# First half's operands made in small pieces between sums, one more sum between two products of each chunk, and two of eight sums on ScalarE in one stage

## The chip, the cores and the metric

The kernel runs on one core of a Trainium2 chip. The engines are named as in the profile: PE is TensorE (PEld its weight loads), DVE VectorE, ACT ScalarE, POOL GpSimd, SP SyncE, whose queue issues most DMAs. The metric is the device time of one execution in microseconds (us), here the median of several runs.

## The reference

Two branches read the same normalized input, and their sum with the input is the output. `q`, `k`, `v` and `x` have 2048 rows of 576 columns.

```python
x  = A_q                              # (1, 2048, 576)
xn = layernorm(x)                     # (x - mean) / sqrt(var + 1e-5), no weights
# branch A: a causal filter of 4 taps on k, times v, a long causal convolution by FFT, gated with xn
kv = sum(k_pad[:, t:t + S] * shift_k[:, ks - 1 - t] for t in range(4)) * v
y  = irfft(rfft(pad(kv)) * rfft(pad(ssm_k)))[:S] + kv * ssm_D
# branch B: an FFN with a hidden width of 4608
h  = maximum(xn @ w1, 0) @ w2
out = x + xn * y + h
```

## The kernel before

**FFN on PE.** The 2048 rows are 16 tiles of 128, in two halves of eight tiles, each half two blocks (`b`) of 512 rows. The hidden width is taken 256 columns at a time. Such a chunk of one half is a *quad*, `g`: 0 to 17 for the first half, 18 to 35 for the second. FP32 operands are split into a high and a low part (ACT copies the high part, DVE or POOL subtracts it), and a product takes three matmuls in place of one. The first two quads are plain (`classical`, four chunks of 14 matmuls each). From quad 2 on (`quad`), the four products of a 2 by 2 block matrix are made by seven (Strassen's scheme, Winograd's form): the x side has the operands `00`, `01`, `11` and the differences `s1` to `s4`, the weight side `wa` to `wd` with `sums`. Each `product` is six matmuls of 512 columns, each `rest` (the last 64 of 576 input columns) two. They are written into two banks, `x` and `y` in `quad`, whose contents ACT and DVE pass on: `u2` and `p5` are copies that the next product is added to, and `hidden` makes the rectified high part (`hh`, ACT) and low part (`ll`, DVE).

Between the products stand the eight *units* of the quad before: `open_unit` takes a PSUM buffer (two in turn), `mm2` multiplies 128 rows of the hidden layer with `w2` in twelve matmuls of 288 columns, and DVE adds the result to `acc`, the 128 by 576 sum of that tile. PE works in program order; where it goes on without a wait, DVE, ACT and POOL have been in time.

**First half's operands.** In the two plain quads the x operands are not yet scaled by `rstd`, which is multiplied in when `acc` is added to. Then `scales` makes a row of the 512 `rstd` values of a block: DVE writes four diagonal matrices, PE multiplies them with ones, ACT copies the row. `scaled` multiplies the operands with it, `combined` makes the differences, `made` and `made_rest` split them. All that is recorded between the plain chunks, in long calls.

**The stream.** `conv` is a generator with branch A and the second half's operands. `tick` is called after each group of matmuls, and gives the stream credit (`rate` times the columns); when it is used up, the next step is recorded. The costs `W_*` say how much credit a step takes, a negative yield is a pause in columns. Its stages: the second half's operands (`later_operands`), the filters' transform (64 `prepare` and `first` steps with `wk`), the taps, gate and first transform of `k` and `v` (`tap`, `gate`, `split`, `first` with `wx`), the middle (`spectrum`, `product_of`, `way_back`, all with `m_sb`), and the way out (`wi`). In the stage of the taps every tile costs DVE seven tap instructions, one gate and two splits. `here()` orders the stream's DVE and ACT work behind the last `acc` and `hh`; a scheduler then sets the order of each engine's instructions.

Of the kernel before, what the change touches and what calls it, by code (L numbers as in the profile page):

```python
# [17 lines left out]
P = 128  # L18
S = 2048
D = 576  # L20
# [44 lines left out]
FFN_TOTAL = (QUADS - PLAIN) * 50 * W_MM + (2 * (QUADS - PLAIN) + 1) * BT * W_UNIT  # L65
# [40 lines left out]
def h3_ffn_kernel(ctx: ExitStack, tc, x, k, v, shift_k, ssm_k, ssm_D, w1, w2, fwd, inv, mid, out):  # L106
# [186 lines left out]
    def scales(pool, b):  # L293

        diag = pool.tile([P, BT, P], F32, tag="diag", name=f"diag{b}")
        for i in range(BT):
            with here():
                nc.vector.tensor_scalar(diag[:, i, :], ident, rstd[:, b * BT + i:b * BT + i + 1],
                                        None, op0=OP.mult)
# [4 lines left out]
        row = pool.tile([P, 512], F32, tag=f"row{b}", name=f"row{b}")  # L304
        with here():
            nc.scalar.activation(row, ps, AF.Copy)
        return row

    def scaled(row, *names):
        for o in names:  # L310
            if isinstance(o, int):
                with here():
                    nc.vector.tensor_tensor(xf[o], xf[o], row[:64], OP.mult)
            else:
                for c in range(2):
                    with here():
                        nc.vector.tensor_tensor(xf[o][:, c, :], xf[o][:, c, :], row, OP.mult)

    def made(o, tag=None):
        dst = operand(o, tag)  # L320
        for c in range(2):
            with here():
                split_chunk(dst, c, xf[o][:, c, :])

    def made_rest(b):
        with here():
            split_rest(rest_operand(b), xf[b])

    def combined(pool, *names):
        for c in range(2):  # L330
            with here():
                combine(pool, xf, names, c)
# [172 lines left out]
    def product(ps, w, off, o, start=False):  # L505

        for c in range(2):
# [5 lines left out]
    def rest(ps, g, b, f):  # L513
        matmuls(ps, [(wr[g][:, n, 0, f * P:(f + 1) * P], hl[b]) for n in range(2)], False)
# [10 lines left out]
    def classical(g, b, f, which, n_low):  # L525
# [19 lines left out]
        hidden(g, b, f, ps)  # L545

    def quad(g, units):
# [16 lines left out]
        product(x, wa[g], 0, "00", start=True)  # L564
# [5 lines left out]
        product(x, wa[g], 2, "01")  # L570
# [7 lines left out]
        product(y, wb[g], 0, "s2")  # L578
# [533 lines left out]
```

## Time and profile before

| | us |
|---|---|
| median of 3 runs | 1096.05 |
| lowest, highest | 1095.46, 1096.5 |
| the profiled execution | 1097.09 |
| its span | 1095.0 |
| PE, PEld busy | 1051.7, 870.8 |
| DVE, ACT, POOL busy | 769.9, 485.5, 457.8 |

The profile is of one execution. Of each engine it tells when an instruction ran, how long the engine sat idle before it, and which instruction on another engine ended that wait. Records of PE overlap, so a PE that is busy need not be at its peak, and the length of a stretch says more than its busy time. Quad 2 starts when PE has done the last plain chunk, at 62.25 us, quad 3 at 99.88. The stage of the filters lies in quads 10 to 15, that of the taps in 16 to 25 (to about 717 us), the middle in 27 to 32.

### The profile page before, as it was taken

To read this page: it belongs to the slowest core of one execution; us is meant where nothing else is said; L and a number is where in the kernel's file an instruction comes from. 1 tells how busy PE (TensorE), PEld (TensorE's weight loads), DVE (VectorE), ACT (ScalarE), POOL (GpSimd) and SP (SyncE) were. 2 spreads that over 40 slices of the span, in tenths; PEclk is the share of its full clock that TensorE was granted. 3 is DMA by queue.
4 is the path that set the end of the run, shared out by engine and by line. 5 is a ranking of instruction groups with operands and counts; after the bars stand their busy time and mean duration, and the time that the engine had idled before them with its cause. 6 is when DMAs were issued, how large, how long until landed. Compare 5 with 4: busy or idle time off the path is not lost. (4 is left out here: it accounts for less than half of the span.)

```text
span 1095.0 us, 17070 instructions
## 1 busy us (share of the span) xinstructions
PE 1051.7 (96%) x6300; PEld 870.8 (80%) x6300; DVE 769.9 (70%) x1149; ACT 485.5 (44%) x929; POOL 457.8 (42%) x496
## 2 busy tenths in 40 slices
PE   8878999999999999798999999999999999999998
PEld 5766899999899998697899899895666665677777
DVE  5787768554887774999999999853444454446765
ACT  7342344333687774344444445434444444432220
POOL 3343454444354444454444445443223223244450
PEclk9989999999999999999999999999999999999999
DMA  6118544992254445589944433237566666457684
GB/s 166 58 38 187 144 150 183 197 154 56 89 160 139 140 140 160 153 259 349 279 134 138 137 114 120 78 138 194 174 197 208 189 209 203 131 179 223 220 248 119
DMA packets 118431, 179.45 MB, mean 164 GB/s; under 512 B 66381, under 2 KB 67551, under 8 KB 116556
## 3 DMA queue, kind: packets, MB, share of 16 engines
q1 hardware_dynamic: 99212, 121.99, 39.3%
q0 software_dynamic: 18816, 55.49, 17.0%
q10 hardware_dynamic: 320, 0.88, 0.3%
q8 instruction: 50, 0.82, 0.3%
q14 instruction: 33, 0.27, 0.1%
HBM read 123.27 MB, written 45.61 MB: 154 GB/s over the span
## 5 line engine op out<-in xcount | busy, mean ns | idle before, releaser
L501 PE MATMUL pso<-w,hh 128*128 128x288 f32 x2304 | 471.4, 297 | 5.4 <-DVE acc L652 3.3
L501 PEld LDWEIGHTS pso<-w,hh 128*128 128x128 f32 x2304 | 381.1, 189 | 36.2 <-issue 8.2
L501 PE MATMUL pso<-w,ll 128*128 128x288 f32 x1152 | 340.4, 295 | 0.0
L656 DVE TENSOR_TENSOR acc<-pso,acc 128x576 f32<-128x576 f32 x272 | 204.6, 753 | 158.0 <-PE pso L501 156.7
L501 PEld LDWEIGHTS pso<-w,ll 128*128 128x128 f32 x1152 | 217.1, 188 | 0.0
L445 POOL TENSOR_TENSOR w<-r,w 128x576 fp32r<-128x576 f32 x72 | 111.5, 1552 | 134.6 <-ACT w L444 134.5
L445 POOL TENSOR_TENSOR wb<-sums,wb 128x512 fp32r<-128x512 f32 x34 | 49.8, 1465 | 203.8 <-ACT wb L444 140.9
L501 PE MATMUL psh<-x,wa 128*128 128x512 f32 x408 | 109.0, 402 | 10.8 <-DVE ll L522 6.5
L501 PE MATMUL psh<-xs,wb 128*128 128x512 f32 x408 | 108.7, 400 | 1.2 <-ACT u L581 1.2
L501 PEld LDWEIGHTS psh<-x,wa 128*128 128x128 f32 x408 | 74.7, 190 | 32.6 <-issue 12.7
L501 PEld LDWEIGHTS psh<-xs,wb 128*128 128x128 f32 x408 | 72.9, 189 | 25.0 <-issue 11.7
L501 PE MATMUL psh<-hl,wr 128*128 128x512 f32 x272 | 88.1, 401 | 1.5 <-ACT psh L604 1.5
L521 ACT ACTIVATE hh<-psh 128x512 fp32r<-128x512 f32 x68 | 40.6, 598 | 91.0 <-PE psh L501 90.7
L604 ACT ACTIVATE psh<-psh 128x512 f32<-128x512 f32 x34 | 19.9, 584 | 132.7 <-DVE u L602 132.7
L445 POOL TENSOR_TENSOR wd<-r,wd 128x256 fp32r<-128x256 f32 x36 | 31.7, 881 | 97.1 <-ACT wd L444 97.1
L522 DVE SCALAR_TENSOR_TENSOR ll<-psh,hh 128x512 fp32r<-128x512 f32 x68 | 46.6, 685 | 34.1 <-ACT hh L521 33.7
L868 DVE TENSOR_TENSOR k<-psf,k 128x512 f32<-128x512 f32 x72 | 44.7, 682 | 36.5 <-PE psf L687 31.6
L676 DVE TENSOR_TENSOR ks<-kt,ks 64x288 fp32r<-64x288 f32 x64 | 54.5, 852 | 18.1 <-ACT ks L675 17.0
L445 POOL TENSOR_TENSOR wa<-r,wa 128x512 fp32r<-128x512 f32 x36 | 51.5, 1430 | 28.8 <-ACT wa L444 28.7
L501 PEld LDWEIGHTS psh<-hl,wr 128*128 128x128 f32 x272 | 46.9, 188 | 19.2 <-issue 12.3
L521 ACT ACTIVATE hh<-p 128x512 fp32r<-128x512 f32 x34 | 21.5, 632 | 90.4 <-DVE p L611 65.4
L501 PE MATMUL psh<-xs,wc 128*128 128x512 f32 x204 | 53.3, 396 | 8.1 <-DVE ll L522 8.1
(146 smaller groups left out, 1642.8 us busy)
## 6 DMA issues: line engine op xcount, KB each, us to landing
r<-in_w POOLq DMA_DIRECT2D x70, 288.0 KB, 3.5
r<-in_w POOLq DMA_DIRECT2D x35, 512.0 KB, 5.2
zk<-zk SPq DMA_DIRECT2D x32, 288.0 KB, 2.6
zx<-zx SPq DMA_DIRECT2D x32, 288.0 KB, 2.7
ztk<-zk SPq DMA_DIRECT2D x18, 512.0 KB, 3.9
ztx<-zx SPq DMA_DIRECT2D x18, 512.0 KB, 3.9
k<-k SPq DMA_DIRECT2D x72, 128.0 KB, 3.2
zy<-vo SPq DMA_DIRECT2D x18, 512.0 KB, 2.6
```

Source lines behind the costliest of these rows:

```text
L445: nc.gpsimd.tensor_tensor(w[:, 1, :n], src, w[:, 0, :n], OP.subtract)
L501: last = nc.tensor.matmul(ps, a, m, start=start and n == 0, stop=n == len(seq) - 1, skip_group_check=True)
L521: done["act"] = nc.scalar.activation(hh, ps, AF.Relu)
L522: nc.vector.scalar_tensor_tensor(ll, ps, 0.0, hh, op0=OP.max, op1=OP.subtract)
L604: nc.scalar.activation(x, y, AF.Copy, scale=-1.0)
L656: done["acc"] = nc.vector.tensor_tensor(two(acc[t]), ps[:, :, :NH], two(acc[t]), OP.add)
L676: nc.vector.tensor_tensor(dst[other], src[own], dst[own], OP.subtract)
L868: nc.vector.tensor_tensor(filt[n][c][:, k, :], banks[k], filt[n][c][:, k, :], OP.mult)
```

## The change

Five things are changed.

1. The eight diagonals are made ahead of the first unit, in buffers of the tag `xn`. The matrix products for the rows stand after two units and after the first chunk of quad 1. The six remaining units of quad 0 stand around the second chunk of quad 1.
2. Scaling, differences and splits of the first half's operands are a generator, `second_half_of_start`, that yields after each piece. `post` records one or two pieces after each unit, four after a plain chunk, until quad 2 is done; `need` records what a product of quad 2 reads ahead of it. Quad 2 is inside the pool `fa` now, so the stream starts after it, one quad later.
3. In every quad unit 3 stands between the products `s2` and `s1`, and unit 4 between `s1` and `s3`.
4. From the stage of the taps up to the middle, units 3 and 4 are *seeded*: ACT copies `acc` into the PSUM buffer, the matmuls add to it, and ACT copies the sum back. DVE has no part in it. There are 26 such units.
5. The stream's costs and pauses have other values.

```diff
-W_FK, W_FX, W_FMK, W_FMX, W_FMB, W_FO = 2.5, 5.8, 2.4, 4.8, 3.4, 6.6
+W_FK, W_FX, W_FMK, W_FMX, W_FMB, W_FO = 2.35, 6.6, 2.4, 4.4, 3.0, 6.0
-KT_GAP = 6000
-N_FB, W_FB = 37, 3.9
+KT_GAP = 4500
+N_FB, W_FB = 37, 4.0
-FFN_TOTAL = (QUADS - PLAIN) * 50 * W_MM + (2 * (QUADS - PLAIN) + 1) * BT * W_UNIT
+FFN_TOTAL = (QUADS - PLAIN - 1) * 50 * W_MM + 2 * (QUADS - PLAIN) * BT * W_UNIT
...
+    def second_half_of_start(pool):
+        for o, b in (("11", 1), ("10", 1), ("00", 0), ("01", 0), (0, 0)):
+            yield from scaled(o, b)
+        yield from combined(pool, "s1")
+        yield from made("s1")
+        yield "00"
+        yield from made("00")
+        yield from combined(pool, "s2")
+        yield from made("s2")
+        yield from made("01")
+        yield from made_rest(0)
+        yield from combined(pool, "s3")
+        yield from made("s3")
+        yield from combined(pool, "s4")
+        yield "10"
+        yield from made("s4")
+        yield from scaled(1, 1)
+        yield from made("11")
+        yield from made_rest(1)
+    def need(g, o):
+        while g == PLAIN and o not in ready:
+            post(1)
...
         def unit(n):
             if n + 1 < len(units):
-                open_unit(*units[n + 1])
+                open_unit(*units[n + 1], n + 1 in stage["seeded"] and more)
             mm2(*units[n])
+            post(2)
...
         nc.scalar.activation(u2, y, AF.Copy)
+        unit(3)
         x = bank(g, 0, "5")
-        product(x, wc[g], 2, "s1", start=True)
+        product(x, wc[g], 2, "s1", start=True, g=g)
...
-        unit(3)
-        product(y, wb[g], 2, "s3")
+        unit(4)
+        product(y, wb[g], 2, "s3", g=g)
...
-        unit(4)
         rest(x, g, b0, 1)
...
+        if seed:
+            seeded.add(t)
+            nc.scalar.activation(ps[:, :, :NH], two(acc[t]), AF.Copy)
...
-            matmuls(ps[:, h, :NH], seq, True)
-        if g < PLAIN:
+            matmuls(ps[:, h, :NH], seq, t not in seeded)
+        if t in seeded:
+            done["act"] = nc.scalar.activation(two(acc[t]), ps[:, :, :NH], AF.Copy)
+            seeded.remove(t)
+        elif g < PLAIN:
...
         with tc.tile_pool(name="fx", bufs=2) as fp:
+            stage["seeded"] = (3, 4)
...
-            yield -2.5 * PAUSE
+            yield -3 * PAUSE
...
         with tc.tile_pool(name="fm", bufs=2) as fp:
+            stage["seeded"] = ()
...
-            yield -1.5 * PAUSE
+            yield -2 * PAUSE
```

DVE at the change from quad 1 to quad 2, before: `ll1_1_0` and `ll1_1_1` are the low parts of quad 1's last two chunks, `x..`, `xs..` and `hl..` pieces of operands, `xf..` differences, `acc..<-pso1_0` the sum of quad 2's first unit.

```order
L203 TENSOR_TENSOR hl0_632<-xfr0_231,hl0_632 64x512
L457 TENSOR_TENSOR sums2_662<-r1_2_420 128x256 x2
L221 TENSOR_TENSOR xf10_335<-xf10_335,xf00_227 128x512 x2
L207 TENSOR_TENSOR xs1_567<-xfs1_564,xs1_567 128x512
L313 TENSOR_TENSOR xfr1_339<-xfr1_339,row1_558 64x512
L207 TENSOR_TENSOR xs1_567<-xfs1_564,xs1_567 128x512
L207 TENSOR_TENSOR xs2_635<-xfs2_619,xs2_635 128x512 x2
L522 SCALAR_TENSOR_TENSOR ll1_1_0_656<-psh1_c10_640,hh1_1_0_655 128x512
L221 TENSOR_TENSOR xf01_229<-xf01_229,xfs2_619 128x512 x2
L457 TENSOR_TENSOR sums2_662<-sums2_662,r1_2_420 128x256
L522 SCALAR_TENSOR_TENSOR ll1_1_1_686<-psh1_c11_670,hh1_1_1_685 128x512
L207 TENSOR_TENSOR x11_713<-xf11_337,x11_713 128x512 x2
```

And DVE at the same place in the changed program.

```order
L573 SCALAR_TENSOR_TENSOR ll1_1_0_629<-psh1_c10_613,hh1_1_0_628 128x512
L207 TENSOR_TENSOR xs1_633<-xfs1_611,xs1_633 128x512
L506 TENSOR_TENSOR sums2_641<-sums2_641,r1_2_420 128x256
L207 TENSOR_TENSOR xs1_633<-xfs1_611,xs1_633 128x512
L573 SCALAR_TENSOR_TENSOR ll1_1_1_665<-psh1_c11_649,hh1_1_1_664 128x512
L207 TENSOR_TENSOR x00_668<-xf00_227,x00_668 128x512 x2
L715 SCALAR_TENSOR_TENSOR acc0_100<-pso1_0_688,rstd_84,acc0_100 128x576
L207 TENSOR_TENSOR xs2_710<-xfs2_673,xs2_710 128x512 x2
L715 SCALAR_TENSOR_TENSOR acc0_100<-pso1_1_696,rstd_84,acc0_100 128x576
L207 TENSOR_TENSOR x01_732<-xf01_229,x01_732 128x512 x2
L203 TENSOR_TENSOR hl0_743<-xfr0_231,hl0_743 64x512
L573 SCALAR_TENSOR_TENSOR ll2_0_0_749<-psh2_1_686,hh2_0_0_748 128x512
```

The pieces of `00`, `s2`, `01` and `hl0` now stand behind `ll1_1_1` and between the sums of quad 2's units.

DVE at the start of the stage of the taps, before: `k-1` and so on are rows ahead of the sequence, `c0` and `e0_1` the first taps of tile 0, which read the loaded `k0` and `sk`; `u2_15` and `p5_15` belong to quad 15.

```order
L758 MEMSET k-3_4278 1x576
L602 TENSOR_TENSOR u2_15_4520<-psh15_5_4522,u2_15_4520 128x512
L656 TENSOR_TENSOR acc4_111<-pso14_5_4570,acc4_111 128x576
L769 TENSOR_TENSOR c0_4481<-k0_4259,sk_4258 128x576
L522 SCALAR_TENSOR_TENSOR ll15_0_1_4603<-u2_15_4520,hh15_0_1_4602 128x512
L656 TENSOR_TENSOR acc6_118<-pso14_6_4606,acc6_118 128x576
L611 TENSOR_TENSOR p5_15_4532<-psh15_2_4438,p5_15_4532 128x512
```

And DVE at the start of that stage in the changed program, where it lies in quad 16.

```order
L822 MEMSET k-3_4298 1x576
L719 TENSOR_TENSOR acc2_103<-pso15_2_4713,acc2_103 128x576
L506 TENSOR_TENSOR sums17_4865<-r1_17_4652 128x256 x2
L833 TENSOR_TENSOR c0_4533<-k0_4279,sk_4278 128x576
L506 TENSOR_TENSOR sums17_4865<-sums17_4865,r1_17_4652 128x256 x2
L836 TENSOR_TENSOR e0_1_4561<-k-1_4288,sk_4278 128x576
L837 TENSOR_TENSOR c0_4533<-c0_4533,e0_1_4561 128x576
L836 TENSOR_TENSOR e0_2_4582<-k-2_4293,sk_4278 128x576
L656 TENSOR_TENSOR u2_16_4788<-psh16_5_4812,u2_16_4788 128x512
```

The first tap has moved ahead of `u2`, and the sums of units 3 and 4 (`pso15_3`, `pso15_4`) are gone from DVE.

ACT in the changed program, at the beginning of quad 16: `pso15_3<-acc2` is a seed, `acc2<-pso15_3` the copy back, `zk31` the last output of the filters' stage.

```order
L620 ACTIVATE psh16_2_4684<-psh16_1_4683 128x512
L693 ACTIVATE pso15_3_4745<-acc2_103 128x2x288
L746 ACTIVATE zk31_4241<-psf_4242 128x288
L746 ACTIVATE zk31_4241<-psf_4265 128x288
L572 ACTIVATE hh16_0_0_4741<-psh16_1_4683 128x512
```

There is no seed before the change; the copies of `zk31` now follow one.

More of the change, by code (lines that the diff above doesn't have):

```diff
@@ L1037, in unit @@
             mm2(0, b, i)
[L1039 to L1042 removed]
+        diag = [diagonal(fa, b) for b in range(2)]
+        unit(0, 0)
+        unit(0, 1)
+        scales(fa, 1, diag[1])
         classical(1, 0, 0, 0, 0)
[L1044 to L1045 removed]
+        scales(fa, 0, diag[0])
+        posts["at"] = second_half_of_start(fa)
+        unit(0, 2)
+        post(1)
+        unit(0, 3)
+        post(1)
+        classical(1, 0, 1, 1, 0, "00")
         for j in range(FT):
```

116 lines of the change are left out of this document (60 added, 56 removed).

## The prediction

> **What bounds the kernel now.** I read the page first, then a table of windows cut at the starts of the quads, then the timeline of PE, DVE, ACT and SP where a window is longer than its work.
>
> ```profile
> PE 1051.7 (96%) x6300; PEld 870.8 (80%) x6300; DVE 769.9 (70%) x1149; ACT 485.5 (44%) x929; POOL 457.8 (42%) x496
> ...
> PE 22%; DVE 0%; issue 0%
> ```
>
> PE is busy 96% of the span, and the chain that ended last is PE's. The change leaves the matmuls as they are, so what it can win or lose are the times in which PE waits, or runs at a lower clock. The windows show where those are (stretch, length, then busy time of PE, PEld, DVE, ACT and POOL, the granted clock, DMA):
>
> ```profile
> 62.25:99.88 37.63, 27.16 (x146) 22.95 (x146) 30.59 (x61) 11.88 (x22) 14.66 (x13) 0.91 0.42 112
> 99.88:127.19 27.31, 24.98 (x148) 22.21 (x147) 20.88 (x42) 8.74 (x18) 11.30 (x12) 1.00 0.78 165
> 410.59:471.89 61.30, 53.85 (x314) 48.09 (x312) 46.13 (x65) 25.23 (x51) 27.12 (x28) 0.97 0.59 155
> 471.89:717.39 245.50, 238.26 (x1435) 216.38 (x1434) 234.25 (x301) 111.22 (x223) 119.52 (x122) 0.99 0.56 177
> 717.39:741.64 24.25, 24.25 (x147) 22.11 (x146) 11.35 (x18) 8.05 (x15) 12.20 (x14) 1.00 0.41 143
> ...
> 417.79 0.69 PE L682 MATMUL psf<-ks,wk 128*128 128x288 f32 x4
> 418.32 0.43 PE L501 MATMUL pso<-w,hh 128*128 128x288 f32 x2
> ```
>
> The last window is quad 26, with no stream work in it: 24.25 us for 146 matmuls. Four matmuls of the stream add 0.53 us (417.79 to 418.32), 0.13 each. So quad 2 (62.25 to 99.88) loses 37.63 - 24.25 = 13.4 us and quad 3 loses 3.1. Quads 15 and 16 (410.59 to 471.89, 20 stream matmuls) lose 61.30 - 48.5 - 2.6 = 10.2. Quads 17 to 25 (120 stream matmuls) lose 245.50 - 218.25 - 15.6 = 11.6, with DVE busy 234 of 245 us: there DVE sets the pace. The single waits:
>
> ```profile
> 39.09 1.12 PE L302 MATMUL psf<-diag,ones 128*128 128x512 f32 x2 [1.69 <-DVE diag L298]
> ...
> 48.30 1.12 PE L302 MATMUL psf<-diag,ones 128*128 128x512 f32 x2 [1.69 <-DVE diag L298]
> ...
> 68.80 2.90 PE L501 MATMUL psh<-x,wa 128*128 128x512 f32 x6 [6.55 <-DVE ll L522]
> ...
> 439.52 0.73 PE L501 MATMUL psh<-x,wa 128*128 128x512 f32 x2 [2.65 <-DVE p L611]
> ...
> 455.81 1.66 PE L501 MATMUL psh<-xs,wc 128*128 128x512 f32 x6 [3.57 <-DVE ll L522]
> ...
> 496.35 0.74 PE L501 MATMUL psh<-hl,wr 128*128 128x512 f32 x2 [1.47 <-ACT psh L604]
> ...
> 497.99 0.54 PE L501 MATMUL pso<-w,hh 128*128 128x288 f32 x2 [0.37 <-DVE acc L656]
> ...
> 500.64 2.14 PE L501 MATMUL psh<-x,wc 128*128 128x512 f32 x6
> ...
> 508.17 1.54 PE L501 MATMUL psh<-x,wa 128*128 128x512 f32 x6
> 509.55 0.62 PE L501 MATMUL psh<-hl,wr 128*128 128x512 f32 x2
> 510.00 0.43 PE L501 MATMUL pso<-w,hh 128*128 128x288 f32 x2
> ...
> 511.60 1.56 PE L501 MATMUL psh<-xs,wb 128*128 128x512 f32 x6
> ```
>
> Each names DVE, or ACT behind DVE. The last rows give the steps at full clock: a product of six matmuls 1.38 us (508.17 to 509.55), the two of `rest` 0.45, a unit of twelve 1.60 (510.00 to 511.60). Some waits also cost clock: after the one of 1.47 us a unit takes 2.65 (497.99 to 500.64) and the next six matmuls 2.14 in place of 1.54, together some 1.6 us for one such drop; after 3.57 us they take 1.66.
>
> **The change part by part.** Prices of DVE and ACT:
>
> ```profile
> L656 DVE TENSOR_TENSOR acc<-pso,acc 128x576 f32<-128x576 f32 x272 | 204.6, 753 | 158.0 <-PE pso L501 156.7
> ...
> L444 ACT ACTIVATE w<-r 128x576 fp32r<-128x576 f32 x72 | 48.2, 678 | 0.2
> ...
> L652 DVE SCALAR_TENSOR_TENSOR acc<-pso,rstd,acc 128x576 f32<-128x576 f32 x16 | 12.9, 809 | 5.0 <-PE pso L501 5.0
> ...
> L522 DVE SCALAR_TENSOR_TENSOR ll<-psh,hh 128x512 fp32r<-128x512 f32 x68 | 46.6, 685 | 34.1 <-ACT hh L521 33.7
> ...
> L521 ACT ACTIVATE hh<-psh 128x512 fp32r<-128x512 f32 x68 | 40.6, 598 | 91.0 <-PE psh L501 90.7
> ...
> L604 ACT ACTIVATE psh<-psh 128x512 f32<-128x512 f32 x34 | 19.9, 584 | 132.7 <-DVE u L602 132.7
> ...
> 61.04 2.27 DVE L457 TENSOR_TENSOR sums<-r 128x256 f32<-128x256 f32 x2
> ...
> 70.72 1.27 DVE L207 TENSOR_TENSOR x<-xf,x 128x512 fp32r<-128x512 f32 x2
> ...
> 116.11 0.75 DVE L457 TENSOR_TENSOR sums<-r 128x256 f32<-128x256 f32 x2
> ...
> 60.34 1.83 POOL L445 TENSOR_TENSOR wa<-r,wa 128x512 fp32r<-128x512 f32 x1 [11.78 <-ACT wa L444]
> ```
>
> *Diagonals.* The eight diagonal pieces now stand ahead of the first accumulations, while PE still works, and each `scales` product follows a unit or a chunk. PE's two waits of 1.69 us go: gain 3.4. What is late next, the scaling of `xf`, is needed only in quad 2.
>
> *Quad 2.* Before, nine pieces of operands stand on DVE ahead of `ll1_1_0`, whose bank quad 2 writes first, and PE waits 6.55 us, with a clock of 0.91 over the window. Afterwards they stand between the sums, and PE meets them one by one. A piece takes 0.64 us (1.27 for two), an `acc` sum 0.81, ends 1.05 after its unit with 0.24 for the signal, and a product ends 0.46 (two matmuls) behind its last piece. (a) `x00`: ACT's `hh` and DVE's `ll1_1_1` (0.2 + 0.6 + 0.68), two pieces (1.27) and 0.46 end 3.2 us after quad 1's last chunk; the product alone is 1.4: 1.8 lost. (b) `x01` and `hl0` stand behind the second sum: 1.05 + 1.27 + 0.68 + 0.46 = 3.4 against 1.84: 1.6 lost. (c) `s4` stands behind the fifth sum: 1.05, two of `xf01`, two sums of weights, a piece, a sum, a piece (1.27 + 0.84 + 0.64 + 0.42 + 0.64), then 0.46: 5.2 against 3.2: 2.0 lost. (d) `hl1` stands behind two units' sums, `xfr1`, `ll2_0_1` and both `x11`: 6.7 us after `s4`, against two units of 3.2: 3.4 lost. Sum 8.8. POOL splits weights meanwhile: two sums of weights take 2.27 us beside POOL's 1.83 at 60.34, and 0.75 where POOL is quiet; I add 0.9 (0 to 9.9, all 13 pieces of (a) to (d) drawn out by 0.76 each). One drop of the clock adds 1.6. So 11.3 lost against 13.4: gain 2.1 (-7 to +5). [...]
>
> *Quad 3.* Its waits (3.1 lost) come from the other half's operands starting there with DVE still behind; those start now a quad later, and nothing in DVE's order is late: 0.6 lost, gain 2.5 (1 to 3).
>
> *Start of the stage of taps (quads 15 and 16).*
>
> ```profile
> 424.50 0.71 ACT L683 ACTIVATE zk<-psf 128x288 f32<-128x288 f32 x2 [1.03 <-PE psf L682]
> ...
> 428.15 0.37 SPq L751 DMA_DIRECT2D sk<-in_shift_k  x1
> ...
> 436.84 0.76 DVE L769 TENSOR_TENSOR c<-k,sk 128x576 f32<-128x576 f32 x1 [4.68 <-DMA k<-in_k]
> ...
> 447.51 0.76 DVE L769 TENSOR_TENSOR c<-k,sk 128x576 f32<-128x576 f32 x1 [0.77 <-DMA k<-in_k]
> ```
>
> The loads of the taps start 2.9 us after ACT's last `zk` (425.21 to 428.15); the first tap runs 8.7 us after that, the tap of the second tile 19.4. DVE stands still 4.68 us for it. In the changed order two things move against PE: a seed that waits for DVE's sum of unit 1 stands ahead of the last `zk` (some 2.5 us), and the first tap stands ahead of `u2_16`, not behind it. I count from the start of quad 16: the last `zk` ends at 7.5, loads at 10.5, first tap at 19.2, `u2_16` done at 23.8, ACT's copy at 24.5; PE wants that at 20.9 and loses 3.6. The second tile's tap lands at 29.9, `p5_16` behind it ends at 33.5, and PE wants the bank at 28.7: 5.0. With 0.4 for unit 7 and one drop of the clock (1.6): 10.6 against 10.2, a loss of 0.4 (-6 to +6). [...]
>
> *Seeds (quads 16 to 28).* Of 26 units the sum leaves DVE (0.753 each, 19.6 us, 15 of them in the ten quads of the stage). ACT gets 52 copies instead; none such is in the trace, so between 0.58 (512 columns of PSUM) and 0.68 (576 of SBUF), I take 0.65: 34 us, 2.6 in a quad of 27, on an engine busy 111 of 245. Also unit 3 now stands between `s2` and `s1`: the product `s1` waited for `ll` (455.81 is one), and gets 1.6 us of cover; the price is that `p5` keeps 3.0 us of cover instead of 4.6 for a copy of 0.6. Against it, the seed of unit 4 stands behind `p5` and `zx` in a few quads, 1 us late each. Of the 11.6 lost I leave 7: gain 4.6 (-4 to +10).
>
> *Denser stages.* The stream's credit is 971.9 / 1,502,013 per column before and 993.2 / 1,462,984 after, from the constants. A quad of 53,248 columns is 24.25 us, so the slot of the filters' transforms falls from 1.76 to 1.58 us, and that of the middle's product from 3.38 to 2.95.
>
> ```profile
> L868 DVE TENSOR_TENSOR k<-psf,k 128x512 f32<-128x512 f32 x72 | 44.7, 682 | 36.5 <-PE psf L687 31.6 <-DMA k<-k 4.9
> ...
> L676 DVE TENSOR_TENSOR ks<-kt,ks 64x288 fp32r<-64x288 f32 x64 | 54.5, 852 | 18.1 <-ACT ks L675 17.0
> ```
>
> The middle's product takes DVE four of 0.682, 2.73: slack falls from 0.65 to 0.22, below one `acc` sum. Eighteen times the lost 0.43 is 7.7 at most; a third, 2.4 lost (0 to 7.7). In the filters' stage DVE's 0.852 fits 1.58: 1 lost (0 to 4). `kt` still has three quads to land.
>
> *Sum:* 3.4 + 2.1 + 2.5 - 0.4 + 4.6 - 2.4 - 1.0 = 8.8. The profiled execution took 1097.09 (span 1095.0 and 2.09 around it), 1.0 over the median of 1096.05. 1097.09 - 8.8 = 1088.3: I forecast **1088** for the median.
>
> **The rivals.** *Slower: the seeds stall PE.* A seeded unit starts only after DVE's sum of two units earlier, then ACT's queue, then the seed; where ACT waits for a gate on DVE (`xs8`, `xs12` stand ahead of a seed), PE waits for both. Price: 26 units times the wait, instead of the 4.6. With 0.7 us each (one seed) the time is 1088 + 4.6 + 18.2 = 1111; from 0.17 us each the gain of the start (8.0) is used up with the rest. For it: DVE 95% busy in that stage; against: unit 2 and the product `s2` (3 us) lie between. *Faster: PE's waits fall away.* If DVE's relief removes the 11.6 and quad 2 loses only the 8.8: 1088 - 7.0 - 2.5 = 1079. For it: the relief of 15 exceeds the 11.6. *No change: the denser middle takes it back.* The whole 7.7 and 4 in place of 3.4: 1088 + 8.3 = 1096. For it: the slack is less than a sum; against: PE is full in that stage now.
>
> **How the numbers follow.** Forecast 0.50 (1081 to 1093), faster rival 0.20, no change 0.12, slower rival 0.18. A difference of 0.2%, 2.2 us, is about what a measurement can tell. Of the forecast's 0.50, 0.02 lies within that of the old time and 0.01 above; of the rival of no change, 0.11 and 0.01. So faster is 0.47 + 0.20 = 0.67, same 0.13, slower 0.20. The range goes from 4 us below the faster rival, 1075, up to 1102, which leaves out about half of the slower rival and the ends of the faster one, some 0.15 together.
>
> **What would show it.** Right: no wait before the `diag` products; quad 2 near 35.5 us with four waits of 1.6 to 3.4 us; quad 3 below 25; a wait of DVE for `k` of over 6 us ahead of `u2_16`, then PE waits of some 3.6 and 5; quads 17 to 25 losing 7. Wrong: seeds waited for by PE, a wait of over 1 us in the middle's every step, or quad 2 longer than 38 us.

## The result and the profile after

The changed kernel takes 1102.75 us (median of 6 runs, 1099.11 to 1104.37) against 1095.77 (6 runs, 1095.17 to 1096.58) for the kernel before. The ratio is 1.0059, with a 95% interval of 1.0043 to 1.0075: 0.6% slower, where I had forecast 0.7% faster. The first rows to read are the page's busy times and the chain of the changed kernel.

```profile
PE 1058.1 (96%) x6300; PEld 876.5 (80%) x6300; DVE 748.8 (68%) x1123; ACT 516.2 (47%) x981; POOL 456.2 (41%) x496
...
PE 80%; DVE 9%; DMA 6%; ACT 3%; issue 2%; SPq 0%; ACTq 0%; DVEq 0%
```

The view of the cores gives span and mean granted clock, here before and then after the change:

```profile
core 0: 1095.0 us, clock 0.991
```

```profile
core 0: 1102.2 us, clock 0.985
```

PE is busy 6.4 us longer for the same 6300 recorded instructions (1058.1 against 1051.7), while the span less PE's busy time only rises from 43.3 to 44.1. The clock tells why: it was 0.991 over the span of 1095.0 before, which is 9.9 us lost, and is 0.985 here, 16.5 lost. So PE waits about as long in all as it did, but in other places, and the clock falls to 0.50 more often, in seven stretches in place of five. The profiled execution is the longest of the six (1104.37); the other five have a clock of 0.987 to 0.991, so the loss to the clock is smaller in them. The two chains cannot be set side by side: that of the kernel before, which the prediction read as PE's alone, was followed over the last 22% of the span only, and this one goes over all of it, through DVE, ACT and DMAs.

Where the time went is read from windows with equal work on both sides. Those of the changed kernel are quad 2 (from the end of the last plain chunk on), quad 3, quads 4 to 9, quad 7 alone, quads 10 to 19 (184 matmuls of the stream) and quads 20 to 26 (72); the columns are those of the prediction.

```profile
58.95:97.60 38.65, 29.99 (x147) 25.52 (x147) 26.31 (x37) 16.34 (x31) 16.30 (x16) 0.87 0.23 64
97.60:121.86 24.26, 24.26 (x147) 22.10 (x146) 17.50 (x43) 7.22 (x14) 10.08 (x11) 1.00 0.48 142
121.86:276.19 154.33, 148.52 (x877) 134.69 (x876) 99.27 (x160) 58.03 (x110) 72.48 (x75) 0.98 0.76 158
196.26:227.63 31.37, 26.63 (x147) 24.07 (x146) 20.02 (x29) 11.28 (x22) 14.47 (x16) 0.89 0.46 158
276.19:567.22 291.03, 275.10 (x1645) 249.09 (x1644) 230.29 (x310) 177.38 (x339) 131.85 (x144) 0.98 0.59 178
567.22:747.87 180.65, 179.83 (x1096) 164.24 (x1095) 153.93 (x202) 98.35 (x189) 89.75 (x92) 1.00 0.38 115
```

The kernel before, quads 4 to 9, 10 to 19 and 20 to 26:

```profile
127.19:272.67 145.48, 145.48 (x878) 132.66 (x876) 91.92 (x140) 57.91 (x109) 73.24 (x75) 1.00 0.67 149
272.67:557.78 285.11, 273.25 (x1645) 248.38 (x1644) 240.60 (x326) 165.47 (x319) 131.62 (x143) 0.99 0.60 184
557.78:741.64 183.86, 180.49 (x1095) 164.23 (x1094) 161.28 (x210) 81.03 (x162) 92.12 (x93) 1.00 0.38 120
```

| stretch | before | after | change | predicted |
|---|---|---|---|---|
| to the start of quad 2 | 62.25 | 58.95 | -3.3 | -3.4 |
| quad 2 | 37.63 | 38.65 | +1.0 | -2.1 |
| quad 3 | 27.31 | 24.26 | -3.1 | -2.5 |
| quads 4 to 9 | 145.48 | 154.33 | +8.9 | none |
| quads 10 to 19 | 285.11 | 291.03 | +5.9 | +1.4, and the seeds' -4.6 |
| quads 20 to 26 | 183.86 | 180.65 | -3.2 | (in the line above) |
| from quad 27 to the end | 353.35 | 354.35 | +1.0 | +2.4 |
| sum | 1095.0 | 1102.2 | +7.2 | -8.8 |

PE's own rows show the largest waits (the timeline of the changed kernel): five ahead of products of quad 2 and one ahead of its rest, one in quad 7, one in quad 16.

```profile
60.22 0.51 PE L550 MATMUL psh<-x,wa 128*128 128x512 f32 x1 [1.26 <-ACT x L206]
61.25 1.64 PE L550 MATMUL psh<-x,wa 128*128 128x512 f32 x5 [0.53 <-DVE x L207]
...
69.21 1.42 PE L550 MATMUL psh<-x,wa 128*128 128x512 f32 x5 [1.58 <-DVE x L207]
...
80.96 0.50 PE L550 MATMUL psh<-xs,wd 128*128 128x512 f32 x1 [0.33 <-ACT xs L206]
82.17 1.66 PE L550 MATMUL psh<-xs,wd 128*128 128x512 f32 x5 [0.71 <-DVE xs L207]
...
91.27 1.22 PE L550 MATMUL psh<-hl,wr 128*128 128x512 f32 x2 [4.24 <-DVE hl L203]
...
221.56 1.22 PE L550 MATMUL psh<-hl,wr 128*128 128x512 f32 x2 [4.74 <-ACT psh L658]
...
467.40 1.22 PE L550 MATMUL psh<-hl,wr 128*128 128x512 f32 x2 [5.60 <-ACT psh L658]
```

The wait at 221.56 is in a quad that ran without one before, and no line of my sum stands for it. This is what ACT, DVE and the two DMA queues do ahead of it (`stgs` is the buffer in which the second half's operands are staged, `ops_s` its copy in HBM, `r` a weight load):

```profile
205.77 1.15 ACT L206 ACTIVATE stgs<-yf 128x512 fp32r<-128x512 f32 x2 [0.59 <-DMA ops<-stg]
206.43 3.25 DVE L207 TENSOR_TENSOR stgs<-yf,stgs 128x512 fp32r<-128x512 f32 x2 [0.28 <-ACT stgs L206]
209.08 1.10 POOL L486 DMA_DIRECT2D r<-in_w  x2
209.71 10.59 SPq L455 DMA_DIRECT2D ops_s<-stgs  x2
...
218.00 1.15 ACT L206 ACTIVATE stgs<-yf 128x512 fp32r<-128x512 f32 x2 [8.54 <-DMA ops_s<-stgs]
218.66 1.29 DVE L207 TENSOR_TENSOR stgs<-yf,stgs 128x512 fp32r<-128x512 f32 x2 [5.86 <-ACT stgs L206]
...
220.93 0.58 ACT L658 ACTIVATE psh<-psh 128x512 f32<-128x512 f32 x1 [1.78 <-DVE u L656]
```

And the same place before the change:

```profile
188.02 1.10 POOL L437 DMA_DIRECT2D r<-in_w  x2
...
191.19 8.05 SPq L406 DMA_DIRECT2D ops_s<-stgs  x2
...
195.60 1.14 ACT L206 ACTIVATE stgs<-yf 128x512 fp32r<-128x512 f32 x2
```

There is one staging buffer. Before, the store of `s3` was issued 3.2 us after the weight loads, and ACT could split `s4` 4.4 us later without a wait. Afterwards it is issued 0.6 us after the loads. ACT, whose work is in order, stands 8.54 us for it, DVE stands behind ACT's split, `u2` behind DVE, the copy of a bank (L658) behind `u2`, and PE behind the copy. PE waits 4.74 us, and quad 7, which takes 24.25 where PE does not wait, takes 31.37 at a clock of 0.89, so some 3.5 us of it are clock. The store issued ahead of that one, at 184.88, held ACT for 6.54 us as well, and quad 6, in which that falls, lost 1.2 us.

The wait in quad 16 is read from DVE (`c` and `e` are the first taps, `u` is `u2_16`):

```profile
458.50 0.76 DVE L833 TENSOR_TENSOR c<-k,sk 128x576 f32<-128x576 f32 x1 [5.39 <-DMA k<-in_k]
...
462.41 0.76 DVE L836 TENSOR_TENSOR e<-k-1_4288,sk 128x576 f32<-128x576 f32 x1 [2.36 <-DMA k-1_4288<-in_k]
...
465.38 0.76 DVE L836 TENSOR_TENSOR e<-k-2_4293,sk 128x576 f32<-128x576 f32 x1 [1.42 <-DMA k-2_4293<-in_k]
466.05 0.68 DVE L656 TENSOR_TENSOR u<-psh,u 128x512 f32<-128x512 f32 x1
```

DVE stands 9.2 us in all for rows of `k` ahead of `u2_16`.

### The profile page after: what moved, and what is told of

It reads as the page before. It is cut to its first block, busy times and chain, and to the rows that moved or that the text cites. A ratio compares the mean times of both kernels' runs of the same rounds, so it can differ in the third digit from the quotient of the medians.

```text
span 1102.2 us, 17117 instructions
## 1 busy us (share of the span) xinstructions
PE 1058.1 (96%) x6300; PEld 876.5 (80%) x6300; DVE 748.8 (68%) x1123; ACT 516.2 (47%) x981; POOL 456.2 (41%) x496
## 4 chain that ended last, share of the span: by engine, by line
PE 80%; DVE 9%; DMA 6%; ACT 3%; issue 2%; SPq 0%; ACTq 0%; DVEq 0%
PE pso L550 36%; PE psh L550 31%; PE psf L750 9%; PE psf L745 3%; DMA ops_s<-stgs 1%; DVE c L837 1%; PE psh_c L550 1%; DMA v<-in_v 1%; DVE acc L719 1%; DVE e L836 1%; DMA sk<-in_shift_k 1%; DMA acc<-in_x 1%; DVE ll L573 1%; DMA k-3_4298<-in_k 1%; DMA ops<-stg 1%
## 5 line engine op out<-in xcount | busy, mean ns | idle before, releaser
L719 DVE TENSOR_TENSOR acc<-pso,acc 128x576 f32<-128x576 f32 x246 | 185.3, 754 | 153.9 <-PE pso L550 151.6
L494 POOL TENSOR_TENSOR w<-r,w 128x576 fp32r<-128x576 f32 x72 | 106.9, 1488 | 144.3 <-ACT w L493 144.0
L550 PEld LDWEIGHTS psh<-hl,wr 128*128 128x128 f32 x272 | 48.6, 190 | 35.1 <-ACT psh L658 14.6
L658 ACT ACTIVATE psh<-psh 128x512 f32<-128x512 f32 x34 | 19.8, 583 | 102.7 <-DVE u L656 102.7
L550 PE MATMUL psh<-xs,wd 128*128 128x512 f32 x204 | 54.8, 397 | 1.0 <-DVE xs L207 0.7
```

The source lines that it names most:

```text
L494: nc.gpsimd.tensor_tensor(w[:, 1, :n], src, w[:, 0, :n], OP.subtract)
L550: last = nc.tensor.matmul(ps, a, m, start=start and n == 0, stop=n == len(seq) - 1, skip_group_check=True)
L658: nc.scalar.activation(x, y, AF.Copy, scale=-1.0)
L719: done["acc"] = nc.vector.tensor_tensor(two(acc[t]), ps[:, :, :NH], two(acc[t]), OP.add)
```

## The experiments

The runs below are given with one table of their profiled executions: the start of quad 3, the lengths of quads 3 to 9, of quads 10 to 26 (256 matmuls of the stream, except where marked), and of the rest to the end. The ratio is that to the kernel before, measured beside each run (medians of 1095.3 to 1095.9), with its 95% interval.

| run | median us | ratio | quad 3 at | 3 to 9 | 10 to 26 | rest |
|---|---|---|---|---|---|---|
| before | 1095.8 | | 99.9 | 172.8 | 469.0 | 353.4 |
| after | 1102.75 | 1.0059 [1.0043, 1.0075] | 97.6 | 178.6 | 471.7 | 354.4 |
| chunk stores | 1092.47 | 0.9971 [0.9959, 0.9983] | 95.8 | 170.6 | 470.5 | 353.2 |
| spacing 4.1 | 1094.84 | 0.9995 [0.9985, 1.0006] | 95.0 | 169.8 | 475.1 | 353.3 |
| no seeds | 1102.02 | 1.0057 [1.004, 1.0073] | 97.3 | 178.3 | 472.3 | 354.0 |
| taps later | 1110.98 | 1.0143 [1.0126, 1.0159] | 94.9 | 178.7 | 475.3 | 359.1 |
| rest first | 1101.57 | 1.0054 [1.0039, 1.0069] | 96.2 | 178.4 | 470.4 | 352.9 |
| loads first | 1100.67 | 1.0049 [1.0033, 1.0065] | 97.4 | 170.5 | 473.9 | 356.9 |
| rest forced | 1092.24 | 0.9971 [0.9957, 0.9985] | 97.3 | 170.3 | 471.8 | 353.2 |
| old units | 1104.67 | 1.0088 [1.0073, 1.0103] | 100.4 | 174.7 | 474.3 | 353.7 |
| old units, no seeds | 1109.51 | 1.0131 [1.0114, 1.0148] | 100.4 | 174.7 | 478.2 | 354.6 |
| before, new units | 1091.44 | 0.9973 [0.9963, 0.9984] | 100.6 | 169.8 | 471.5 (272) | 347.4 |
| seeds late | 1092.97 | 0.9976 [0.9966, 0.9985] | 92.8 | 170.4 | 469.7 | 354.1 |
| seeds later | 1094.38 | 0.9979 [0.9962, 0.9996] | 96.8 | 170.7 | 472.7 | 354.4 |
| gap 3900 | 1091.8 | 0.9953 [0.9937, 0.997] | 95.7 | 170.3 | 472.3 | 350.8 |
| gap 4200 | 1095.88 | 1.0006 [0.9993, 1.0019] | 97.2 | 170.4 | 478.7 | 351.7 |
| gap 3900, no seeds | 1084.09 | 0.9894 [0.9878, 0.9911] | 95.2 | 170.4 | 465.0 | 350.7 |
| the same, seeds from tile 2 | 1089.45 | 0.9947 [0.9925, 0.9969] | 92.8 | 170.5 | 473.6 | 350.8 |
| the same, seeds from tile 0 | 1086.39 | 0.992 [0.9903, 0.9937] | 94.6 | 170.6 | 471.0 | 351.0 |

**The staging buffer.** Two runs, each on the changed kernel.

```diff
-            dst = pool.tile([P, 2, 2, 512], F32R, tag="stg", name=f"stg{o}")
             for c in range(2):
+                dst = pool.tile([P, 2, D], F32, tag="xn", name=f"stg{o}_{c}", bufs=3)
...
+                nc.sync.dma_start(ops_n[o][:, :, c, :], dst[:, :, 0, :].bitcast(F32))
```

> The changed kernel, but each of the second half's operands is staged and stored in two chunks that go round three buffers, in place of one buffer of 1 MB (ACT's split no longer waits for the store just issued). Theory (staging): quads 4 to 9 lose 8.9 us more than before because ACT, in order, stands 8.5 us behind a store that met the weight loads; then the wait of 4.7 us of PE in quad 7 goes, quads 4 to 9 take 145.5 to 147 us in place of 154.3, and the time falls by 7 to 9 us, to 1094 to 1096, and scatters less than 1099 to 1104. Rival (DVE beside POOL): what is late there are DVE's pieces that run at 1.6 us in place of 0.65 beside POOL; then quads 4 to 9 stay above 152 and the time within 2 us of the changed kernel's.

```diff
-N_FB, W_FB = 37, 4.0
+N_FB, W_FB = 37, 4.1
```

> The changed kernel with one number changed: a step of the second half's operands costs 4.1 credits in place of 4.0, which is 6017 columns a step, as before the change (6027), in place of 5892. One staging buffer, as before. Theory (phase): the stall of quad 7 comes from the steps' spacing; 37 steps of 130 columns more put the store of s3 2.2 us later against the quad, behind the weight loads as it was before the change; PE's wait of 4.7 us goes, quads 4 to 9 lose under 2 us in place of 8.8, and the time is 1094 to 1097. Rival (the stream's later start is enough): with one buffer a stall of over 4 us stays somewhere in quads 4 to 9, and the time stays at 1100 to 1104.

Quads 4 to 9 in the window views of the two runs, chunk stores and then spacing, and from the timeline of the second ACT's split behind the store:

```profile
120.04:266.35 146.31, 145.83 (x878) 132.66 (x876) 100.96 (x160) 58.16 (x110) 72.44 (x75) 1.00 0.81 167
```

```profile
119.30:264.86 145.56, 145.56 (x878) 132.63 (x877) 101.18 (x161) 57.54 (x108) 72.81 (x75) 1.00 0.77 168
```

```profile
212.41 1.16 ACT L206 ACTIVATE stgs<-yf 128x512 fp32r<-128x512 f32 x2 [0.60 <-DMA ops_s<-stgs]
```

Both theories were right on the six quads. With three buffers that are each half as large, they take 146.31 in place of 154.33 and the kernel 1092.47, below the 1094 to 1096 expected; with one buffer and steps that cost 2.5% more (6017 columns in place of 5892) they take 145.56 and the kernel 1094.84, ACT waiting 0.60 for the same store. So the stall needs the single buffer and the place that the tighter steps give the store. The start a quad later is not enough for it, and the new numbers (with 4.0 a step is 5892 columns, before it was 6027) had moved that store.

**Edits that did not move what they named.** Three runs:

```diff
-            yield -3 * PAUSE
+            yield -4 * PAUSE
```

> The changed kernel with a pause of 4 in place of 3 (16000 columns, 7.3 us, longer) ahead of the first tap. Theory (DVE in order): PE's wait of 5.6 us in quad 16 comes from u2_16 standing on DVE behind a tap whose rows have not landed; then u2_16 goes ahead of it, that wait and the clock's drop behind it are gone, quads 16 and 17 lose about 5 in place of 13, and the time falls by 4 to 8 us; what is left are 120 columns' worth of later taps. Rival (the loss moves on): the same taps then stand ahead of quad 17's u2 or p5, with a new wait of over 3 us there, and the time changes by less than 2 us.

```diff
-        yield from made("11")
         yield from made_rest(1)
+        yield from made("11")
```

> The changed kernel, but the last pieces of quad 2 in another order: hl1 ahead of the two pieces of x11. Theory (order): PE's wait of 4.24 us for hl1 in quad 2 falls to 1.5 to 2 us, the clock's drop behind it goes too, quad 2 takes 35 to 36.5 us in place of 38.8, and the time falls by 2 to 4 us. Rival (x11 is late in its turn): PE waits as long at the last product, and quad 2 stays at 38 us or more.

The third records the loads of `v` and of the first two matrices `wx` halfway through the pause:

```diff
+            yield -1.5 * PAUSE
+            for t in range(2):
+                load_more(t)
+            yield -1.5 * PAUSE
```

> The kernel of the chunk stores (1092.5), with the loads at the start of the taps in another order: sk and k of the first taps first; v and the matrices wx of the first two tiles, 1.1 MB, half of the pause later. Theory (loads share 200 GB/s): the rows of the first taps land 2 to 4 us earlier, DVE's waits for them and with them PE's wait of 4.4 us in quad 16 fall to 0 to 2.5 us, quads 16 and 17 lose 7 to 10 in place of 13.5, and the time falls to 1087 to 1090. Rival (the taps' own work holds u2): the rows land earlier but PE waits as long, or a matrix is late; 1091 to 1094.

With the longer pause DVE's order around the first tap is the same, row for row: the tap is recorded later, but the scheduler apparently puts an instruction where it takes its operands to be ready. PE's wait was 4.27 us; what did change is the end, where PE's last matmul ended at 1097.87 and the stream's last outputs only at 1108.0. The rest first was the same miss: `hl1` stayed behind both pieces of `x11`, and PE waited 4.25. With the loads in another order the two `wx` still went out with `k`, only `v` moved, PE waited 3.85 and 3.10 in quad 16, and the end came 8.5 us after PE's last matmul in place of 5.1. Two of the three ended outside both of the times expected (1110.98 and 1100.67). They test no theory of mine; they say that a change of recording order has to be looked up in the engines' order before it is called an experiment.

**The rest forced.** On the chunk stores, with an edge on DVE from `hl1` to both pieces of `x11`:

```diff
+            with tc.issue_after(low.ins):
+                split_chunk(dst, c, xf["11"][:, c, :])
```

> The kernel of the chunk stores, and in quad 2 both pieces of x11 held on DVE behind hl1 by an edge (the recording order alone had not moved them). Theory (order): PE's wait of 4.24 us for hl1 falls by the two pieces, to 2.0 to 3.0 us, x11 then lies under quad 2's last unit, and quad 2 is 1.2 to 3 us shorter; the time is 1089.5 to 1091.5. Rival (x11 late in its turn): the last product waits for what hl1 no longer does; 1092 to 1094.

Quad 2 of this run, and of the run with seeds late, whose program is the same up to there:

```profile
59.13:97.28 38.15, 30.37 (x147) 25.72 (x147) 26.17 (x37) 16.03 (x31) 16.39 (x16) 0.87 0.21 59
```

```profile
58.93:92.83 33.90, 26.11 (x148) 21.98 (x148) 26.10 (x37) 16.04 (x31) 15.37 (x15) 1.00 0.15 48
```

The wait for `hl1` is 3.05 us in place of 4.24, just above the 2.0 to 3.0 that I expected, and the median did not move (1092.24 against 1092.47). The two rows tell why a microsecond cannot be seen here: with the same instructions and the same waits of PE (within 0.01 us), one execution of quad 2 takes 4.25 us longer than the other, and what differs is the clock, 0.87 against 1.00. Over the eight runs that share this program the start of quad 3 lies between 92.8 and 97.3.

**Units.** On the chunk stores, units 3 and 4 go back to their old places; then that without seeds; and the kernel before with only the new places.

```diff
-        unit(3)
         x = bank(g, 0, "5")
...
+        unit(3)
         product(y, wb[g], 2, "s3", g=g)
...
+        unit(4)
         rest(x, g, b0, 1)
```

> The kernel of the chunk stores, with units 3 and 4 back in their places of before (behind the product s1 and behind s3); seeds as they are. In this order u2_16 stands ahead of the first tap on DVE. Theory (the new places put u2 behind taps): PE's wait of 4.4 us in quad 16 is gone, and quads 15 to 18 lose 3 us less or more; but the product s1 waits again for ll in some quads of the stage of the taps, 1 to 3.5 us each. If the new places of the units are a gain in all, the time rises by 2 to 6 us, to 1094.5 to 1098.5; rival (they are the loss): it falls to 1086 to 1090.

> The kernel of the chunk stores with units 3 and 4 in their places of before and no seeds: what is left of the change is the new first phase, the stream's start a quad later, and the numbers. In quads 16 to 19, which take 118.3 us before the change with 56 of the stream's matmuls and 125 to 126 after it: if the loss there comes from units and seeds together, they are back at 118 to 120 for 56 matmuls; rival (the stage meets another place in its quad, with rows that land 17 us into quad 16 where they landed 26 us into quad 15), they stay at 122 to 126. The time, from the run with the old places (1104.7) and the one without seeds, is 1100 to 1106 in either case, since the waits for ll are back.

> The kernel before, with one part of the change: unit 3 between the products s2 and s1, unit 4 between s1 and s3. Theory (a gain for itself): the product s1 no longer waits for ll, which are 7.1 us of single waits in the kernel before (3.57, 1.56, 1.39, 0.91 in the stage of the taps, 0.71 in quad 3) with one drop of the clock less; the time falls by 3 to 8 us, to 1088 to 1093. Rival (p5 and u2 have less cover): it stays within 2 us, or the scheduler places the taps worse and it rises.

Of the run with the old places, the wait of the product `s1` for `ll` in quad 4:

```profile
137.35 2.93 PE L551 MATMUL psh<-xs,wc 128*128 128x512 f32 x6 [2.48 <-DVE ll L574]
```

The new places are a gain, and a larger one than expected. With the old ones the new kernel is 12 us slower, where 2 to 6 were expected: in the profiled executions quad 3 starts 4.6 later, quads 3 to 9 take 4.2 more, quads 10 to 26 3.8, and the rest 0.5. Of the 4.6, some 1.7 are clock ahead of any moved unit (0.57 from 62 to 66 us, against 1.00 in the chunk stores), so they are no effect of the places. PE's wait of 4.4 us in quad 16 was gone, as expected, but one of 2.91 us for a sum stood in that quad. Put into the kernel before, the new places are worth 0.27% (0.16 to 0.37), about 3 us, but in the profiled execution not where I expected it: less 0.1325 us for each of the 16 more matmuls of the stream, quads 10 to 26 take 469.4 in place of 469.0, and the gain is in quads 3 to 9 (3.0) and behind quad 26 (3.9 with those matmuls counted there), for reasons that these runs do not isolate. In my sum the places were a clause inside the term of the seeds. Without seeds and with the old places quads 16 to 19 took 123.9 us for 58 matmuls where the kernel before took 118.3 for 56, so the loss at the start of the taps needs neither the seeds nor the new places; the rival held there, while the time, 1109.51, lies above the 1100 to 1106 expected.

**Seeds and the start of the taps.** On the changed kernel the seeds are switched off; on the forced rest they begin late, and later.

```diff
-            stage["seeded"] = (3, 4)
```

> The changed kernel without seeds: units 3 and 4 are added by DVE everywhere, everything else is kept. Theory (seeds help a little, late): DVE gets 26 sums back, the later quads of the stage of the taps lose 3 to 5 us more, its first quads stay as they are; the time rises by 2 to 5 us. Rival (seeds stall PE at the start of the stage): the waits of PE for sums and copies in quads 16 to 18 go, and the time falls by 3 us or more.

> The kernel of the forced rest (chunk stores, hl1 ahead of x11; 1092.2), with seeds from the second tile's taps on in place of the stage's beginning: two seeds fewer, and on DVE u2_16 now stands behind two taps instead of four. Theory (a seed by its place): the seeds of the stage's first quads let the scheduler move taps ahead of u2_16, those later relieve DVE; so quads 15 and 16 lose 3 to 6 us in place of 9.0, quads 17 to 26 keep their loss of 15, and the time is 1086 to 1090. Rival (the loss moves on, as in the run without seeds): what quad 16 no longer loses quads 17 and 18 do, and the time is 1091 to 1094.

> As the run before, with seeds from the first transform of tile 0 on: three seeds fewer, and u2_16 stands behind one tap. Theory (a seed by its place): PE's wait in quad 16 is below 3 us, quads 15 and 16 lose 3 to 5 us, and the time is 1085 to 1089. Rival (the loss moves on): 1091 to 1094.

Quads 10 to 19 and 20 to 26 without seeds (here 176 and 80 matmuls of the stream):

```profile
275.59:565.07 289.48, 275.24 (x1637) 249.64 (x1636) 234.28 (x316) 163.79 (x313) 129.33 (x142) 0.98 0.58 175
565.07:747.88 182.81, 181.38 (x1104) 165.38 (x1103) 167.11 (x220) 84.73 (x167) 93.42 (x93) 1.00 0.40 120
```

Without seeds the two stretches are 472.29 in place of 471.68, and the time is 1102.02 in place of 1102.75, neither of the two times expected: 18.1 us less work for DVE (748.8 busy against 766.9) are worth nothing that can be told apart. With the old places of the units the seeds do pay: 1104.67 with them and 1109.51 without, and the intervals of the two ratios do not meet. Beginning late or later gave 1092.97 and 1094.38 against 1092.24; the loss moved on, as the rivals had it.

Then the place of the stage was moved by the pause between the loads of `kt`. With 3900, `u2_15` and `p5_15` stand ahead of the first tap on DVE; with 4500 `u2_16` stands behind four instructions of taps, with 4200 behind six.

```diff
-KT_GAP = 4500
+KT_GAP = 3900
```

> The kernel of the forced rest (chunk stores, hl1 ahead of x11; 1092.2), with one number changed: the pause between the loads of kt is 3900 columns in place of 4500 (6000 before the change). The whole stream then stands some 10 us earlier against the quads, the stage of the taps begins in the middle of quad 15, and on DVE u2_15 and p5_15 stand ahead of the first tap. Seeds and the places of the units are kept. Theory (place in the quad): the start of the taps costs more after the change because its rows land between unit 2 and unit 5, ahead of u2; at the new place quads 15 to 19 lose 14 to 18 us in place of 22.8, and the time is 1084 to 1088. Rival (seeds or the places of the units cost it, wherever the stage begins): they lose 21 to 24 and the time is 1090.5 to 1094.

> The run before without seeds. Theory (seeds relieve DVE where nothing waits for rows): with the stage at a place where no tap stands ahead of u2, seeds are worth the 15 us of DVE's time in part, and without them the time is 2 to 6 us above the run with the pause of 3900. Rival (seeds move the loss and don't remove it): within 1.5 us of it.

> As the run with the pause of 3900, with 4200: the stage begins early in quad 16, and u2_16 stands behind six instructions of taps on DVE, where it is four with 4500. Theory (place in the quad): PE's wait ahead of the rest in quad 16 is as long as or longer than the 5.4 us with 4500, quads 15 to 19 lose 22 to 27 us, and the time is 1092 to 1097. Rival: no dependence on that order, and the time is 1084 to 1090 as the stream is earlier by half.

With 4200, the wait in quad 16:

```profile
461.34 1.22 PE L560 MATMUL psh<-hl,wr 128*128 128x512 f32 x2 [7.17 <-ACT psh L668]
```

Quads 10 to 19 and 20 to 26 (184 and 72 matmuls), with 3900 and seeds, and then without seeds:

```profile
266.02:557.50 291.48, 275.50 (x1645) 248.46 (x1644) 228.40 (x311) 181.52 (x343) 132.76 (x144) 0.98 0.58 177
557.50:738.29 180.79, 179.93 (x1097) 164.27 (x1095) 155.57 (x199) 98.14 (x189) 92.08 (x93) 1.00 0.42 127
```

```profile
265.66:550.51 284.85, 273.38 (x1646) 246.62 (x1645) 232.83 (x322) 168.06 (x319) 132.28 (x143) 0.99 0.58 182
550.51:730.67 180.16, 179.64 (x1096) 164.23 (x1095) 159.03 (x214) 81.82 (x161) 92.55 (x93) 1.00 0.37 115
```

The place alone did not help: quads 15 to 19 lost 21.4 us (length less 24.25 a quad and 0.1325 a matmul of the stream) where I expected 14 to 18, with new waits in quad 16. The rival held. But without seeds, where I had expected 2 to 6 us more, the same place takes 1084.09, 7.7 less, and quads 15 to 19 lose 16.1. This is the fastest kernel of the study, 1.06% under the kernel before (0.89 to 1.22). With 4200 the order decided as expected: 7.17 us of wait where `u2_16` stood behind six instructions of taps, 1095.88.

I then thought that the seeds' cost was DVE's order over the first taps, and gave that kernel seeds behind them:

```diff
             for t in range(T):
+                if t == 2:
+                    stage["seeded"] = (3, 4)
```

> The kernel with the pause of 3900 and no seeds (1084.1), with seeds from the third tile's transforms on, that is from the middle of quad 16: 22 seeds. DVE's order over the first taps is the same as without seeds, up to the second tile's last taps. Theory (order at the start): what the seeds cost is that with them the scheduler puts taps whose rows have not landed ahead of the FFN's instructions; from here on no tap waits for rows, so seeds cost nothing, and relieve DVE: 1081 to 1084.5. Rival (seeds cost wherever they are, as ACT stands behind DVE's sums): 1086 to 1091.

> The same with seeds from the first tile's transforms on: 24 seeds, the first of them in quad 16, while the rows of tile 1 land. ll of quad 15 still stands ahead of the first tap. Theory (order at the start): within 2 us of the run with seeds from the third tile on, 1081 to 1085. Rival (seeds cost wherever they are): 1086 to 1092, and above that run.

Two rows of DVE with seeds from tile 2 on:

```profile
476.21 0.76 DVE L516 TENSOR_TENSOR sums<-r 128x256 f32<-128x256 f32 x2 [1.96 <-DMA r<-in_w]
...
527.63 2.85 DVE L846 TENSOR_TENSOR c<-c,e 128x576 f32<-128x576 f32 x1
```

That theory fell too. With DVE's order over the first taps kept, seeds from tile 2 on cost 5.4 us (1089.45). Seeds from tile 0 on, with which that order is the same only at its beginning, cost 2.3 (1086.39), which the intervals do not tell from either. What the rows show of the first is in quads 17 and 19. Without the sums of two units ahead of them the sums of weights come up on DVE before their load has landed, DVE stands for 1.96 us, `u2_17` follows late, PE waits 2.04 and 1.55 us there, and the clock is 0.97 over quads 10 to 19, against 0.99 without seeds. In quad 19 a tap takes 2.85 us in place of 0.75, for a reason that was not isolated, `ll` stands behind it, and PE waits 2.74. So in this run the time that seeds free on DVE went to waits of DVE and to the clock, but which of them would come at another place cannot be said beforehand from these runs: what the seeds are worth, from a gain of 5 us (old places) to a cost of 8, stays open.

## Why the prediction was wrong, step by step

*Right, or near.* The diagonals: predicted 3.4, measured 3.3, with a wait of 0.60 us left ahead of one `diag` product. Quad 3: predicted 2.5, measured 3.1. The waits of quad 2: (a) 1.8 predicted, 1.79 measured (1.26 and 0.53); (b) 1.6, and 1.58; (c) 2.0, and 1.04; (d) 3.4, and 4.24; in all 8.8 and 8.65. That the sum is so near is luck in part, since (c) and (d) miss in opposite directions; the terms given for (c) add up to 5.3 and not to 5.2. DVE's waits for `k` ahead of `u2_16` are 9.2 us in sum, the longest 5.39, where one of over 6 was expected. PE's wait behind `u2_16`, predicted at 3.6 with another of 5.0, came as one of 5.6 at a clock of 0.90 over quad 16, which is 3.3 us; quads 15 and 16 together lost 9.4, where 10.6 was predicted, so the total is nearer than its parts. The denser middle: 2.4 predicted, 1.0 measured.

*Wrong, first and largest: a step that has no term.* The prediction said of the second half's operands that "those start now a quad later, and nothing in DVE's order is late". I followed DVE and left out what else these steps issue: a store of 1 MB on SP from a single buffer, and ACT's next split behind it. That step, which the sum put at nothing, measured 8.9 of the 16.0 us between forecast and result, and with it removed (chunk stores) the change is a gain of 0.29% (0.17 to 0.41).

*Wrong, second: quad 2's clock.* The waits were right within 0.2 us in sum, but the prediction allowed "One drop of the clock", 1.6 us, and 0.9 for POOL. The window of quad 2 has a clock of 0.87 over 38.65 us, 5.0 lost. That turned a gain of 2.1 into a loss of 1.0, and quad 2 is longer than 38 us, which the prediction had named as a sign of being wrong. In (d) a piece of `x11` took 1.76 us beside POOL's split of `wb`, where two took 1.27 before the change; that is some 1.1 us more for the one, and (d) came 0.84 longer than predicted.

```profile
86.84 1.79 POOL L494 TENSOR_TENSOR wb<-sums,wb 128x512 fp32r<-128x512 f32 x1 [8.26 <-ACT wb L493]
...
87.41 1.76 DVE L207 TENSOR_TENSOR x<-xf,x 128x512 fp32r<-128x512 f32 x1
```

*Wrong, third: the start of the taps and the seeds.* Over quads 10 to 26 I had a gain of 3.2 and the kernel lost 2.7. These are quads 15 and 16 and quads 17 to 25 after the change (32 and 120 matmuls of the stream):

```profile
411.55:473.64 62.09, 55.59 (x326) 50.18 (x324) 37.04 (x55) 34.23 (x67) 25.42 (x29) 0.95 0.60 162
473.64:722.35 248.71, 239.35 (x1434) 216.58 (x1435) 226.41 (x291) 134.95 (x263) 120.96 (x123) 0.99 0.58 178
```

The forecast's "Of the 11.6 lost I leave 7" took DVE's freed time as time that PE gets. DVE is busy 226 us in place of 234 there, and quads 17 to 25 lose 14.6, more than the 11.6 of before, with 13.4 of it in quads 17 to 19 alone (6.8 before). In quads 20 to 26 it looked like a gain (3.2 less), but the run without seeds keeps most of it (length 182.81 with 8 more matmuls of the stream, or 181.75), so it belongs to the units' places and the numbers. My slower rival was seeds that stall PE, at a wait for each seed; PE did wait for a seed's copy (1.3 us in the run with seeds late, 1.8 with 4200), but that is not the price of 7.7 us with 3900: some 3 of it are clock (0.992 over 1089.1 us against 0.995 over 1081.4), and how the rest divides between waits behind DVE and behind ACT was not isolated.

Over the whole kernel 6.6 us more were lost to the clock than before (16.5 against 9.9), where the forecast had one drop of 1.6 us in quad 2 and one in quads 15 and 16.

## What to carry to other kernels

When a change shifts a stream of work against the main loop, list every queue and buffer that each of the shifted steps uses, the stores too, and ask where each now meets the main loop's own transfers; a 2.5% change of a step's cost decided 8.8 us here. Time freed on an engine off the critical path is only a gain if the instructions that the critical engine waits for move up in that engine's order (18.1 us less work for DVE gained nothing here that can be told apart), so predict from the order and not from the busy time. Where waits come close together, as in quad 2, count the clock as a cost of its own, with a scatter as wide as itself: with the same instructions and waits of PE, the longest of 3.05 us, quad 2 took 38.15 us at a clock of 0.87 in one execution and 33.90 at 1.00 in another.

## What the runs showed of the hardware that I had not expected

In quad 2 of the changed kernel the granted clock is 0.50 in two stretches, from 62.30 to 65.70 us and from 89.60 to 96.43, and the same waits are followed by the first in one execution and not in another. These are the same four microseconds of quad 2 in the changed kernel and in the run with seeds late:

```profile
62.00:66.00 4.00, 4.00 (x18) 3.85 (x18) 0.19 (x1) 3.11 (x7) 4.00 (x5) 0.57 0.00 0
```

```profile
62.00:66.00 4.00, 4.00 (x30) 3.83 (x28) 1.50 (x4) 3.61 (x8) 4.00 (x5) 1.00 0.00 0
```

After waits of 1.26 and 0.53 us in the one and of 1.78 and 0.30 us in the other, the first runs 18 matmuls at a mean clock of 0.57 and the second 30 at 1.00. The run with the rest forced has the second's instructions and waits there, and its clock is 0.57 too, over 17 matmuls. From 62.30 to 65.70 us the changed kernel's granted clock is 0.50, so the stretch is 3.4 us long, and it costs 1.7. Waits of 1.79 us together were followed by it here; what decides whether it comes was not shown.

The profile's list of DMAs, for the kernel before, has the store from the staging buffer, 1 MB, at a median of 3.9 us from issue to landing:

```profile
ops_s<-stgs SPq DMA_DIRECT2D x4, 1024.0 KB, 3.9
```

The one that the changed kernel issued 0.6 us after two weight loads (288 KB each) held ACT until 8.3 us after its issue (209.71 to 218.00). The trace has no landing of that store itself, but it has those of the two loads: 4.4 and 8.4 us after their issue, where the two ahead of the store in the kernel before took 3.1 and 3.3.
